# Router columns first: attention's last value columns moved into the steps of a search

## The chip, the core and the metric

The program runs on one core of one Trainium2 chip, as one launch. The metric is device time in microseconds. Below, PE is the matrix engine, DVE the vector engine, ACT the scalar engine, POOL the general engine, SP the queue that issues most transfers.

## What is computed

Three layers in a row, all in f32. Attention: 8 batches, 8 heads, 576 queries of 64 columns; keys and values are averaged over groups of 8 rows, so a query sees 72 of them. A mixture of 8 experts with a greedy assignment under a capacity of 576 tokens each. A gated feed-forward layer.

```python
attn = softmax(scale * q @ pool8(k).T); x = attn @ pool8(v)        # 4608 tokens x 512
logits = x @ w_gate                                                # 4608 x 8
for idx in argsort(-logits.flatten()):       # best pair first
    tok, e = idx // 8, idx % 8
    if assigned[tok] < 0 and counts[e] < 576: assigned[tok] = e; counts[e] += 1
out[mask_e] = relu(x[mask_e] @ w1[e]) @ w2[e]                      # each expert
return (sigmoid(out @ w_gate2) * (out @ w_val2)) @ w_out2
```

## The kernel before

The attention (`attention`, lines 242 to 603) works in 18 tiles of 256 tokens: two for each batch, and behind every fourth batch a mixed one (tiles 8 and 17) with the queries left over from four batches. A tile is cut into chunks of heads (line 294): packed tiles into three of 3, 3 and 2 heads, the first tile and the mixed ones into four of 2. A chunk has u units, one for each head and each of two query rows: 6 or 4. It goes through scores (PE, line 456, several chunks in one group, one score buffer), a maximum and a subtraction (DVE, 472 and 476), exp (ACT, 479), a transpose (PE, 492), a copy to SBUF (ACT, 500), values (PE, 517 and 512; 526 in mixed tiles), and then on DVE the sums (534, 535), the normalisation to `xt` (541) and the logits `lm` (547); the last chunk of a tile adds its logits up into `L` (550), and SP stores `xt` to `x_rows` (559, 563).

The router's logits come out of the same matmul as the values: the right-hand side `wv` has 73 columns for each head, 64 of the value, 8 of value times router weight, and a column of ones for the sum. In packed tiles one value matmul covers two units, so it streams 146 columns over weights of 108 rows and 128 columns (`eT`); a chunk of 6 units has four of them, one of 4 units has two, and a third of 73 columns. An f32 matmul shows as two instructions in the trace.

The order of all this is worked out by a planner, `Plan` (line 155): each piece is an `Op` with a cost for each engine, what it waits for, the buffer it makes and a rank. `Plan.run` takes, among the pieces that can start within 0.25 us of the earliest, the one with the lowest rank. Ranks go by the chunk's number, so the mixed tile 17 comes last. Buffers are counted by tag (line 270): one score buffer, two `aps` for values, four `qps`, three `xt`.

Behind the attention the router takes over. Keys for token columns 0 to 25 are made while the attention runs (598, 599), those of columns 26 to 35, which are tiles 13 to 17, behind it (603). Then come eight phases, one for each expert. In a phase (`Router.phase`, line 924) two searches of four steps each (`search`, 886) look for the threshold: DVE compares the keys with 15 thresholds (`C`), PE counts with 36 small matmuls, DVE finds the hits (`hit`, `fl`), PE turns them into the next thresholds. The generator yields before it counts (with a cost of 0.8) and after the hits (0.05). Behind the last step DVE writes `GE` and `EG`, the expert is chosen, its weights are loaded (`stg`), its slots are worked out and its rows of `x_rows` gathered (`xg`).

The first phase has nothing beside it. `experts` (line 1036) runs it in a loop; from its 17th step on, `heat` puts filler matmuls into PE's waits (lines 1251 to 1256). From the second phase on a search runs between the matmuls of the expert before. The memory of the attention (tile pools `acon`, `alod`, `awrk`, `apsm`) is given back when `attention` ends, and the pools of the experts lie in the same place; `cw` are buffers for the weights of the third layer, which SP starts to load at the start of `experts`.

Of the kernel before, what the change touches and what calls it, by code (L numbers as in the profile page):

```python
# [18 lines left out]
G = S // 8  # L19
N = B * S  # L20
DM = H * D
E = 8
# [132 lines left out]
class Plan(Flow):  # L155
# [9 lines left out]
    def op(self, lanes, f, after=(), reads=(), makes=None, rank=0, size=0, alone=False, rate=350e3, dmas=1):  # L165
        x = Op(lanes, f, [a for a in after if a is not None], list(reads), makes, rank)
        x.size, x.alone, x.rate, x.dmas = size, alone, rate, dmas
# [34 lines left out]
    def run(self):  # L202
        while self.todo:
# [38 lines left out]
def attention(tc, c, q, k, v, w_gate, xD, L, router, scr):  # L242
    nc = tc.nc
    ident = c["ident"]
    with ExitStack() as ctx:
# [24 lines left out]
        BUFS = dict(kv=6, q2=2, qps=4, sps=1, aps=2, mx=3, sd=3, e=7, eT=4, qT=5, rs=3, xt=3)  # L270
# [26 lines left out]
        NQ = len(chunks)  # L297
        fb = {b: first[ti] for ti, (n, b, jj) in enumerate(tiles) if b is not None and jj == 0}
# [106 lines left out]
        def plan_q(ti):  # L405
            n, b, jj = tiles[ti]
            base = first[ti]
# [24 lines left out]
        def plan_score(group):  # L432
# [24 lines left out]
            sc = fl.op({"tensor": 0.3 + 0.125 * at}, score, after=list(dict.fromkeys(need)), reads=read, makes=sps, rank=group[0] - 3)  # L457
            for y in group:
                score_of[y][1] = sc
            return score_of[group[0]]  # L460

        def plan_chunk(y, out):
# [5 lines left out]
            mx, sd, e, tps, eT, aps, rs = (Buf(m, None) for m in ("mx", "sd", "e", "qps", "eT", "aps", "rs"))  # L468
            sps, sc, at = score_of[y] if y in score_of else plan_score(group_of[y])
            S2 = lambda: sps.ap[:, :, G * at:G * (at + nh)].rearrange("p r (h k) -> p r h k", k=G)  # L470
            two = lambda ap: ap.rearrange("p (r h) k -> p r h k", r=2)
            m = fl.op({"vector": 0.07 + 72 * u / 960}, lambda eng: eng.tensor_reduce(tile_of(mx, work, [128, 6])[:, :u].rearrange("p (r h) -> p r h", r=2), S2(), axis=AX.X, op=OP.max),
                      after=[sc], makes=mx, rank=y - 3)
# [4 lines left out]
            s = fl.op({"vector": 0.07 + 72 * u / 960}, sub, after=[m], reads=[sps, mx], makes=sd, rank=y - 3)  # L478
            x = fl.op({"scalar": 0.13 + 72 * u / 1200}, lambda eng: eng.activation(tile_of(e, work, [128, 6, G])[:, :u], sd.ap[:, :u], AF.Exp),
                      after=[s], reads=[sd], makes=e, rank=y)  # L480
# [12 lines left out]
            tn = fl.op({"tensor": 0.109 * len(cuts)}, turn, after=[x], reads=[e], makes=tps, rank=y)  # L493

            def turned(eng):
                t = tile_of(eT, work, [108, 4, 128])
# [4 lines left out]
            tcp = fl.op({"scalar": 0.52}, turned, after=[tn], reads=[tps], makes=eT, rank=y)  # L501

            def values(eng):
                p = tile_of(aps, psum, [128, 6, 73])
                t = eT.ap
                count["av"] += 1
                if packed[ti]:
                    flat = wv[b % 2].rearrange("p w h d -> p (w h) d")
                    for a in range(0, u, 3):
# [28 lines left out]
            def norm(eng):  # L538
                if out.ap is None:
                    out.ap = work.tile([128, 2, H, D], F32, name="xt", bufs=3), work.tile([128, 2, H, E], F32, name="lm", bufs=3)  # L540
# [1297 lines left out]
```

## Time and profile before

| | us |
|---|---|
| median of 3 runs | 1505.7 (1504.81 to 1512.39) |
| the profiled execution | 1506.83 |
| its span | 1505.2 |
| PE busy in it | 1459.1 (97%) |
| DVE busy | 1059.7 (70%) |
| ACT busy | 537.8 (36%) |

The page cuts the span into 40 equal slices and gives the busy tenths of each engine and the clock that PE was granted. The chain that ended last is followed back from the last instruction; windows give busy times by stretch; groups by shape give the mean duration of one instruction. Lines are those of the kernel before; where a helper records the operations, all have line 615, and the tiles tell them apart.

### The profile page before, as it was taken

How to read it: one execution, taken by the hardware profiler on the slowest of the kernel's cores; microseconds unless marked ns; L12 is line 12 of the kernel's file. 1: busy time of each engine (PE TensorE's matmuls, PEld its weight loads, DVE VectorE, ACT ScalarE, POOL GpSimd, SP SyncE). 2: the span in 40 equal slices, each digit the busy share in tenths (PEclk: the TensorE clock that was granted, in tenths of full speed). 3: DMA queues.
4: the chain of work that ended last, by engine and by line, in shares of the span. 5: the costliest groups of instructions: out<-in, count | busy, mean ns of one | idle time of the engine just before them, and what ended most of it. 6: DMA issues, size and time to landing. Idle time of an engine off the chain costs nothing.

```text
span 1505.2 us, 27177 instructions
## 1 busy us (share of the span) xinstructions
PE 1459.1 (97%) x10625; PEld 1309.6 (87%) x10625; DVE 1059.7 (70%) x2344; ACT 537.8 (36%) x1063; POOL 395.5 (26%) x416
## 2 busy tenths in 40 slices
PE   8999799999999999998999999999999999999997
PEld 6898489999999999997888888888888899999996
DVE  6789788988899986247788755577455855574564
ACT  5665143444334444345334322232321322232221
POOL 5682042244333422154324210012000220011001
PEclk9999699999999999999999999999999999999999
DMA  9984336536554775047566564626544375555651
GB/s 331 311 305 140 116 125 211 187 111 210 182 192 134 247 239 188 24 152 292 218 238 227 205 221 150 234 110 231 191 166 182 112 293 192 227 212 226 247 196 43
DMA packets 109329, 294.22 MB, mean 195 GB/s; under 512 B 12588, under 2 KB 43344, under 8 KB 94992
## 3 DMA queue, kind: packets, MB, share of 16 engines
q1 hardware_dynamic: 101636, 270.48, 50.3%
q0 software_dynamic: 6496, 20.98, 4.2%
q8 instruction: 84, 1.38, 0.4%
q10 hardware_dynamic: 1068, 1.03, 0.3%
q14 instruction: 45, 0.37, 0.1%
HBM read 222.33 MB, written 66.08 MB: 192 GB/s over the span
## 4 chain that ended last, share of the span: by engine, by line
PE 82%; DVE 9%; DMA 4%; issue 2%; POOL 1%; SPq 1%; ACT 0%; POOLq 0%; ACTq 0%; DVEq 0%
PE pj L1675 19%; PE hps L615 12%; PE acc L615 12%; PE Yv L1577 7%; PE Yg L1577 7%; PE Zg L1577 5%; PE Xg L1577 5%; PE Xv L1577 5%; PE Zv L1577 5%; DMA kv<-in_v_dram 2%; PE rps L615 2%; PE aps L517 2%; DVE cx L615 1%; PE qps L492 1%; PE sps L456 1%
## 5 line engine op out<-in xcount | busy, mean ns | idle before, releaser
L615 PE MATMUL acc<-hh,w 128*128 128x288 f32 x1024 | 246.1, 305 | 0.0
L615 PE MATMUL hps<-xh,w 128*128 128x288 f32 x1024 | 234.8, 300 | 1.0 <-DVE hl L615 1.0
L1689 DVE TENSOR_TENSOR stg<-pj,stg 128x512 f32<-128x512 f32 x180 | 123.8, 689 | 109.1 <-PE pj L1675 108.2
L615 PEld LDWEIGHTS acc<-hh,w 128*128 128x128 f32 x1024 | 177.1, 189 | 0.2
L615 PEld LDWEIGHTS hps<-xh,w 128*128 128x128 f32 x1024 | 174.5, 189 | 1.9 <-DVE hl L615 1.4
L615 PE MATMUL acc<-hl,w 128*128 128x288 f32 x512 | 151.6, 296 | 0.9 <-DVE hl L615 0.9
L615 PE MATMUL hps<-xl,w 128*128 128x288 f32 x512 | 151.4, 296 | 0.1
L615 POOL TENSOR_TENSOR w<-stg,w 128x512 fp32r<-128x512 f32 (+1 forms) x81 | 119.8, 1493 | 116.0 <-ACT w L615 109.9
L615 ACT ACTIVATE hh<-hps 128x288 fp32r<-128x288 f32 x128 | 52.6, 411 | 252.8 <-PE hps L615 237.8
L1577 PE MATMUL Yg<-w 128*128 128x512 f32 (+1 forms) x540 | 126.5, 369 | 3.7 <-ACT w L1475 3.7
L1577 PE MATMUL Yv<-w 128*128 128x512 f32 (+1 forms) x540 | 126.5, 369 | 0.1
L1577 PEld LDWEIGHTS Yg<-w 128*128 128x128 f32 x540 | 99.6, 188 | 19.9 <-ACT w L1475 4.1
L1577 PEld LDWEIGHTS Yv<-w 128*128 128x128 f32 x540 | 99.5, 189 | 13.6 <-DVE vc L1613 0.8
L615 POOL DMA_INDIRECT xg<-x_rows,idxs x48 | 46.0, 959 | 221.9 <-PE hps L615 70.2
L1675 PE MATMUL pj<-woh,xg 128*128 128x512 f32 x396 | 98.4, 390 | 0.7 <-DVE woh L1544 0.7
L1675 PE MATMUL pj<-woh,cw 128*128 128x512 f32 x396 | 98.7, 390 | 0.0
L615 PEld LDWEIGHTS acc<-hl,w 128*128 128x128 f32 x512 | 97.1, 190 | 1.1 <-DVE hl L615 1.1
L1643 ACT ACTIVATE sg<-sg 128x512 f32<-128x512 f32 (+1 forms) x90 | 53.0, 589 | 122.6 <-DVE sg L1614 73.9
L615 PEld LDWEIGHTS hps<-xl,w 128*128 128x128 f32 x512 | 96.6, 189 | 0.3 <-DVE xl L615 0.3
L615 DVE SCALAR_TENSOR_TENSOR hl<-hps,hh 128x288 fp32r<-128x288 f32 x128 | 57.4, 452 | 53.2 <-ACT hh L615 52.1
L615 ACT ACTIVATE w<-stg 128x512 fp32r<-128x512 f32 (+1 forms) x138 | 81.0, 638 | 34.5 <-DVE rem L615 28.9
L1675 PEld LDWEIGHTS pj<-woh,xg 128*128 128x128 f32 x396 | 74.0, 188 | 15.8 <-DVE woh L1544 1.1
(280 smaller groups left out, 2954.3 us busy)
## 6 DMA issues: line engine op xcount, KB each, us to landing
w<-w_split SPq DMA_DIRECT2D x84, 1024.0 KB
stg<-in_moe_w_dram SPq DMA_DIRECT2D x30, 1024.0 KB
w_split<-w SPq DMA_DIRECT2D x21, 1024.0 KB
woh<-wo_split SPq DMA_DIRECT2D x24, 512.0 KB
wr<-wo_split SPq DMA_DIRECT2D x12, 1024.0 KB
kv<-in_k_dram SPq DMA_DIRECT2D x12, 768.0 KB
kv<-in_v_dram SPq DMA_DIRECT2D x12, 768.0 KB
x_cols<-x SPq DMA_DIRECT2D x16, 576.0 KB
```

Source lines behind the costliest of these rows:

```text
L456: eng.matmul(p[cs, r, G * j:G * j + G], t.ap[rs, h % 4, cs], kpT[rs, b if b is not None else 4 * n + 2 * c + r, h], start=True, stop=True)
L492: eng.transpose(p[:z, j], flat[:, a:a + z], ident)
L517: eng.matmul(p[:, a + s:a + s + 2], t[:, j + s], flat[:, x0:x1 + 1:x1 - x0], start=a + s == 0, stop=True, skip_group_check=True)
L615: r = f(*args, **kw)
L1577: eng.matmul(t, W(a, k), X(b, k), start=first and n == 0, stop=n == 5, skip_group_check=True)
L1643: x = fl.op(A, lambda eng: eng.activation(T(g), T(g), AF.Sigmoid), after=[op], rank=rank)
L1675: eng.matmul(self.tile(ps), G(a), W(b), start=n == 0, stop=n == 5)
L1689: y = fl.op({"vector": 0.69}, lambda eng: eng.tensor_tensor(A(), self.tile(ps), A(), op=OP.add), after=[x, st["acc", u, i]], reads=[ps], r ...
```

## The change

Tiles 13 to 16 (batches 6 and 7) are `halved`. In each of their chunks the values matmul takes the columns 64 to 72 alone, 9 for each unit and so 18 for each matmul, into one `aps` for the whole tile. Sums, reciprocals and logits are then done once for a tile, on 16 units. `eT` of these chunks is kept in buffers of the raw loads (`kv`). The 64 value columns become operations of their own that are marked `late` (`plan_rest`): for each tile 11 matmuls, 16 scalings on ACT (one for each unit, with the reciprocal as scale) and the store. The planner may place them, but it stops when only late ones are left. The rest goes out behind the attention's last piece: matmuls up to the 15th (`burst(15)`), then the keys of columns 26 to 35, then one or two matmuls in each of the fifteen yields of the first phase's two searches, and what is then left at once. Scalings and stores follow their matmuls in the same list.

The mixed tile's ranks are lowered by 6, beside those of tile 15. `xt` has six buffers. The first phase's searches run inside `attention` now, with their PSUM in the `aps` buffers and a pool `router0` of their own on the other side of the memory; `experts` goes on behind them, and `heat` plans its fillers at 0.216 us.

```diff
-        while self.todo:
+        while not all(x.late for x in self.todo):
...
-        BUFS = dict(kv=6, q2=2, qps=4, sps=1, aps=2, mx=3, sd=3, e=7, eT=4, qT=5, rs=3, xt=3)
+        BUFS = dict(kv=6, q2=2, qps=4, sps=1, aps=2, mx=3, sd=3, e=7, eT=4, qT=5, rs=3, xt=6, rl=4)
...
+        rk = lambda y: y - 6 if chunks[y][0] == 17 else y
+        halved = {13, 14, 15, 16}
...
+        def plan_rest(ti, own, rs, out, n2, store):
+            done = []
+            for triples, h0, nh, u, y in pend[ti]:
+                ps, last = Buf("qps", None), n2
+                parts = []
+
+                def one(eng, parts=parts, ps=ps, triples=triples, y=y, nh=nh):
+                    if not parts:
+                        parts.extend(triples(tile_of(ps, psum, [128, 6, 64]), own.part[y], 0, 64, nh))
+                        parts.reverse()
+                    o, i, m, new = parts.pop()
+                    eng.matmul(o, i, m, start=new, stop=True, skip_group_check=True)
+                for j in range(u // 3 * 2 + (u % 3 > 0)):
+                    last = fl.op({"tensor": 0.223}, one, after=[last], makes=ps, rank=500 + y, late=True)
+
+                def scale(eng, ps=ps, h0=h0, nh=nh, u=u):
+                    for a in range(u):
+                        r, h = a // nh, h0 + a % nh
+                        eng.activation(out.ap[0][:, r, h], ps.ap[:, a], AF.Identity, scale=rs.ap[:, r * H + h:r * H + h + 1])
+                done.append(fl.op({"scalar": 0.18 * u}, scale, after=[last], reads=[ps], rank=500 + y, late=True))
+            fl.op({"sync": 0.6}, store, after=done, rank=500, size=524288, late=True)
...
             def values(eng):
+                count["av"] += 1
+                if own:
+                    p = tile_of(aps, psum, [128, 2 * H, 9])
+                    for o, i, m, new in triples(p, own.part[y], 64, 73, H, h0):
+                        eng.matmul(o, i, m, start=new and h0 == 0, stop=True, skip_group_check=True)
+                    return
...
-            av = R["av", y] = fl.op({"tensor": 0.248 * (len(cuts) // 2 * 2) + 0.175 * (len(cuts) % 2) if packed[ti] else u * (0.175 if b is not None else 0.2)}, values,
-                                    after=[tcp] + vals, reads=[eT], makes=aps, rank=y)
+            av = R["av", y] = fl.op({"tensor": 0.115 * len(cuts) if own else 0.248 * (len(cuts) // 2 * 2) + 0.175 * (len(cuts) % 2) if packed[ti] else u * (0.175 if b is not None else 0.2)}, values,
+                                    after=[tcp] + vals, reads=[eT], makes=aps, rank=rk(y))
+
+            if own:
+                pend.setdefault(ti, []).append((triples, h0, nh, u, y))
+                if h0 + nh < H:
+                    return
+                nu, c0, hs = 2 * H, 0, slice(0, H)
...
         fl.run()
         for _ in consts:
             pass
+        rest = deque(fl.todo)
+
+        def burst(n):
+            while rest and (n > 0 or "tensor" not in rest[0].lanes):
+                x = rest.popleft()
+                lane, = x.lanes
+                x.f(getattr(nc, lane))
+                n -= lane == "tensor"
...
+        router.nc, router.psum, router.spare = Clock(nc), Banks, Banks
+        burst(15)
         router.keys(0, 26, 36)
+        router.steps = router.run()
+        for i in range(15):
+            cost, _ = next(router.steps)
+            burst(2 if cost > 0.1 else 1)
+        burst(len(rest))
...
-        rt = router.run()
+        rt = router.steps
...
-        n = 0
         while st["phase"] < 1:
-            n += 1
-            if n > 16:
-                heat(wait["ready"] - 0.1, 0.43 if n < 25 else 0.216)
+            heat(wait["ready"] - 0.1)
             route()
```

## Rows read from the trace of the kernel before

**Rows 1.** The page, section 2: busy tenths in 40 slices; granted clock

```profile
PE   8999799999999999998999999999999999999997
...
PEclk9999699999999999999999999999999999999999
```

**Rows 2.** Windows: stretch, length, busy us of PE, PEld, DVE, ACT, POOL; clock; DMA

```profile
142.00:149.00 7.00, 7.00 (x122) 6.51 (x124) 6.34 (x21) 4.62 (x11) 0.00 (x0) 1.00 0.18 75
...
128.00:159.70 31.70, 28.92 (x467) 25.36 (x467) 27.88 (x101) 17.44 (x40) 0.00 (x0) 1.00 0.29 107
```

**Rows 3.** Chain that ended last, 0 to 260 us: start, us, what

```profile
156.28 0.60 ACT eT L500
156.93 0.73 PE aps L526 x16
...
158.96 0.75 PE aps L526 x16
...
179.62 0.70 PE rps L615 x7
```

**Rows 4.** Timeline of the search: start, us, engine, line, operation, tiles

```profile
165.98 0.20 PE L615 MATMUL rps<-trw,fl 128*128 128x15 bf16 x1 [0.26 <-DVE hit L615]
...
166.67 1.02 PE L615 MATMUL acc<-EoU,C 128*15 128x8 bf16 x35
...
167.95 0.19 PE L615 MATMUL rps<-trw,fl 128*128 128x15 bf16 x1 [0.26 <-DVE hit L615]
```

**Rows 5.** Groups by shape, 128 to 161.2 us: busy us, mean ns; idle before

```profile
L541 DVE TENSOR_TENSOR xt<-aps,rs 128x384 f32<-128x384 f32 x8 | 4.5, 558 | 0.3
...
L541 DVE TENSOR_TENSOR xt<-aps,rs 128x256 f32<-128x256 f32 x8 | 3.4, 424 | 0.2
...
L547 DVE TENSOR_TENSOR lm<-aps,rs 128x48 f32<-128x48 f32 x8 | 1.6, 194 | 0.0
...
L500 ACT ACTIVATE eT<-qps 72x128 f32<-72x128 f32 x4 | 1.1, 264 | 0.0
```

**Rows 6.** Chain around 147 us, then the timeline of weight loads there

```profile
146.78 0.50 PE aps L517 x4
147.28 0.18 PE aps L512 x2
...
147.12 0.19 PEld L512 LDWEIGHTS aps<-wv,eT 72*128 72x128 f32 x1
147.23 0.30 PEld L517 LDWEIGHTS aps<-wv,eT 108*128 108x128 f32 x2
```

**Rows 7.** Timeline behind T0: last logits, last counts of step one

```profile
160.70 0.38 DVE L550 TENSOR_REDUCE L<-lm 128x16 f32<-128x128 f32 x1
...
163.25 0.39 PE L615 MATMUL acc<-EoU,C 128*15 128x8 bf16 x10 [1.70 <-DVE EoU L881]
```

**Rows 8.** Who waited for whom: us in total, times, longest

```profile
SPq L615 <- DMA x_rows<-xt: 1.6, 1, 1.6
...
PE acc L615 <- DVE lm L547: 1.0, 1, 1.0
```

**Rows 9.** Timeline of SP's issues

```profile
160.60 2.45 SPq L563 DMA_DIRECT2D x_rows<-xt  x4
164.99 1.30 SPq L615 DMA_DIRECT2D cw<-in_moe_w_gate_dram  x3
182.45 0.98 SPq L615 DMA_DIRECT2D stg<-in_moe_w_dram  x2
```

**Rows 10.** Timeline at the end of the search

```profile
178.51 0.29 DVE L615 TENSOR_TENSOR GE<-kl,rps 128x36 bf16<-128x36 f32 x2 [0.29 <-PE rps L615]
```

**Rows 11.** Windows of 1 us, columns as in rows 2

```profile
156.00:157.00 1.00, 0.26 (x4) 0.07 (x4) 0.97 (x5) 0.72 (x2) 0.00 (x0) 1.00 0.75 307
...
167.00:168.00 1.00, 0.74 (x29) 0.64 (x25) 0.23 (x3) 0.00 (x0) 0.00 (x0) 0.50 0.93 381
184.00:185.00 1.00, 1.00 (x5) 0.30 (x3) 0.96 (x3) 0.00 (x0) 0.00 (x0) 0.81 0.70 240
```

More of the change, by code (lines that the diff above doesn't have):

```diff
@@ L163, in __init__, with op @@
         self.flights = [0.0] * 8
[L165 removed]
+    def op(self, lanes, f, after=(), reads=(), makes=None, rank=0, size=0, alone=False, rate=350e3, dmas=1, late=False):
         x = Op(lanes, f, [a for a in after if a is not None], list(reads), makes, rank)
[L167 removed]
+        x.size, x.alone, x.rate, x.dmas, x.late = size, alone, rate, dmas, late
         for b in x.reads:
@@ L456, in score @@
                             eng.matmul(p[cs, r, G * j:G * j + G], t.ap[rs, h % 4, cs], kpT[rs, b if b is not None else 4 * n + 2 * c + r, h], start=True, stop=True)
-            sc = fl.op({"tensor": 0.3 + 0.125 * at}, score, after=list(dict.fromkeys(need)), reads=read, makes=sps, rank=group[0] - 3)
+            sc = fl.op({"tensor": 0.3 + 0.125 * at}, score, after=list(dict.fromkeys(need)), reads=read, makes=sps, rank=rk(group[0]) - 3)
             for y in group:
@@ L519, in values @@
+                    for o, i, m, new in triples(p, t, 0, 73, nh):
+                        eng.matmul(o, i, m, start=new, stop=True, skip_group_check=True)
                 else:
@@ new lines, in sums, with begin @@
+            def sums(eng):
+                r = tile_of(rs, work, [128, 2 * H if own else 6])
+                eng.tensor_scalar(r[:, :nu], aps.ap[:, :nu, c0 + 8], 1e-9, None, op0=OP.add)
+                eng.reciprocal(r[:, :nu], r[:, :nu])
+            sm = fl.op({"vector": 0.3}, sums, after=[av], makes=rs, rank=rk(y))
+            def begin():
+                if out.ap is None:
+                    out.ap = work.tile([128, 2, H, D], F32, name="xt", bufs=BUFS["xt"]), work.tile([128, 2, H, E], F32, name="lm", bufs=BUFS["xt"])
@@ L538, in norm @@
             def norm(eng):
-                if out.ap is None:
-                    out.ap = work.tile([128, 2, H, D], F32, name="xt", bufs=3), work.tile([128, 2, H, E], F32, name="lm", bufs=3)
+                begin()
                 eng.tensor_tensor(out.ap[0][:, :, h0:h0 + nh, :], two(aps.ap[:, :u, 0:64]),
                                   rs.ap[:, :u].rearrange("p (r h) -> p r h", r=2)[:, :, :, None].to_broadcast([128, 2, nh, 64]), op=OP.mult)
-            n1 = fl.op({"vector": 0.07 + 64 * u / 960}, norm, after=[sm], makes=out, rank=y)
+            if not own:
+                n1 = fl.op({"vector": 0.07 + 64 * u / 960}, norm, after=[sm], makes=out, rank=rk(y))
@@ L549, in logits @@
                 if h0 + nh == H:
                     eng.tensor_reduce(L[:, 2 * ti:2 * ti + 2, :], lm.rearrange("p r h e -> p r e h"), axis=AX.X, op=OP.add)
-            n2 = fl.op({"vector": 0.12 if h0 + nh < H else 0.45}, logits, after=[n1], reads=[aps, rs], rank=y)
+            n2 = fl.op({"vector": 0.12 if h0 + nh < H else 0.55 if own else 0.45}, logits, after=[sm if own else n1], reads=[aps, rs], makes=out, rank=rk(y))
             if h0 + nh < H:
@@ L564, in store @@
                                       xt[64 * s:64 * s + 64, r].rearrange("p h d -> p (h d)"))
-            fl.op({"sync": 0.6 if b is not None else 2.4}, store, after=[n2], reads=[out], rank=y, size=524288, dmas=1 if b is not None else 4)
+            if own:
+                plan_rest(ti, own, rs, out, n2, store)
+                return
+            fl.op({"sync": 0.6 if b is not None else 2.4}, store, after=[n2], reads=[out], rank=rk(y), size=524288, dmas=1 if b is not None else 4)
         def loads_of(b):
```

71 lines of the change are left out of this document (45 added, 26 removed).

## The prediction

> **What bounds the kernel now.** The page comes first. In its 40 slices of 37.6 us the granted TensorE clock is at 9 tenths or more everywhere but in the fifth, 150 to 188 us, and PE is busy for 8 tenths or more of every slice behind that but the last [rows 1]. The fifth holds the end of the attention and the first search, and the change adds no work behind it. What happens before only moves the rest, so I follow the points that come ahead of it: the last value matmul of the attention (call it T0), the first hit, the last hit, and GE, the first step after the search.
>
> The stretches come second. From 128 us, where the last five tiles begin, to T0 at 159.7 PE is busy 28.9 of 31.7 us, DVE 27.9, ACT 17.4 [rows 2]. From 142 to 149 PE leaves no gap at all [rows 2]. Its gaps lie behind 149. Third, the chain of waits says which: the last tile (17, the mixed one) runs alone, and each of its chunks goes transpose, ACT copy (156.28), values, 2.0 us apart (values at 156.93 and 158.96) [rows 3], PE standing still during the copies. So there are two limits: PE's own work, and the latency of the mixed tile.
>
> Then the first search, from T0 to 178.5. It is a pure latency chain: PE counts, DVE hit, PE threshold, DVE compare, 1.97 us a step (thresholds at 165.98 and 167.95) [rows 4], eight steps. ACT does nothing in it.
>
> **DVE's share.** In tiles 13 to 16 twelve chunks lose their sums, normalisation and logits. That is 8 wide normalisations of 558 ns and 4 narrow ones of 424, for each wide chunk a logit product of 194 [rows 5], and two small operations for the sum. Counted at 1.0 us a wide chunk and 0.85 a narrow one that is 8 x 1.0 + 4 x 0.85 = 11.4 us, against four single sums and products on 16 heads at an estimated 0.6 each: DVE loses about 9 us of its 27.9. It then no longer limits anything before T0. Sixty-four normalisations of 64 columns go to ACT, which is idle in the search; the nearest row, an ACT copy of 128 columns, takes 264 ns [rows 5], so 0.15 to 0.25 us each, 10 to 16 us in a stretch of 18.
>
> **PE's share.** A value matmul goes from 146 moving columns to 18, and one of 128 follows later. What does a short one cost? Each f32 matmul is two passes, each with its own weight load. Four passes over 146 columns take 0.50 us, two over 73 take 0.18 (0.125 and 0.09 a pass) [rows 6]. So half the columns save a quarter. The reason stands in the loads: the load behind the short pass starts 0.11 us after the one before it (147.12, 147.23) [rows 6], however short the pass. I therefore price the 18-column matmul at 2 x 0.11 = 0.22 us against 0.25, and the third one of a narrow chunk at 0.22 against 0.18: 40 x 0.03 - 4 x 0.04 = 1.0 us saved, not the 5.7 that the planner's new cost (0.115 a matmul) assumes. Bounds: 0 and 5.7. The Trainium skill ("TensorE: Matmul & The Clock Gate", section "LDWEIGHTS (loading the stationary operand)") speaks against the change in the same place: a load's time goes by the columns of the weights, by its formula 107 ns for 128. By that rule the estimate would be 0.21 us a matmul and 1.4 us saved; the trace's 0.11 agrees.
>
> The separate matmuls of 128 columns lie between the two rows: 0.23 us, 44 of them, 10.1 us of new PE work.
>
> **T0.** The ranks put the mixed tile beside tiles 15 and 16, so its latency is covered and the gaps behind 149 can be filled. PE's visible idle time from 128 to T0 is 31.7 - 28.9 = 2.8 us; the pipeline's drain after each wait counts as busy too (a threshold matmul of 15 columns shows 0.20 us [rows 4]), so up to about twice that can come back. I take 3.5 and the 1.0 from above. Against that, the late operations stay candidates in the planner's loop: wherever its plan has PE idle for over 0.25 us, it puts one in. Its plan prices the short matmuls at half of what they cost, so some of these gaps won't exist on the chip. I take 8 of the 44 there (bounds 0 and 20), and half of their 1.8 us as a delay. T0 comes 3.5 + 1.0 - 0.9 = 3.6 us earlier; bounds 0.5 and, with the cheap matmul, 8.
>
> **The first hit.** Before, the last counts of the first step run at 163.25, after the keys of columns 26 to 35, which start after the logits at 160.70 [rows 7]. From T0 that is 3.6 us, and PE is nearly free in it. Now 15 late matmuls stand first in PE's order, 15 x 0.23 = 3.45 us, then the 26 counts that need no new keys (0.8, at the pace of [rows 4]), and only then the last ten: at 4.25, 0.7 us later than before. That is the cost of a cover that is almost long enough.
>
> **The steps.** One late matmul stands between the counts and the threshold, two between threshold and counts. The holes are there: from the end of a count group (about 167.69) to the threshold at 167.95 is 0.26 us, against 0.23; from the threshold at 165.98 to the counts at 166.6 is 0.63, against 0.46 and a first load of 0.11 [rows 4]. Cost at full clock: 0, at most 0.1 a step.
>
> **The end of the search.** 36 late matmuls are left at T0 by my count. The first burst and the fifteen steps take 15 + 22 = 37 of them, so the last go out with the last hits. Behind them on ACT come the scales of their chunk, behind these on SP the last store. Who waits for that? The tiles of the next stage lie where the attention's were. The rows show what the first user of such memory waits for: the first load of cw waited 1.6 us for the stores of xt [rows 8]; it was issued at 164.99, 1.9 us after the last of the four stores had been [rows 9]. The first count matmul likewise waited for the last reader of the attention's PSUM [rows 8]. GE is the first write into such a region on DVE, and lies on the path: at 178.51, straight behind the last threshold [rows 10], with the stores landed long before. Now the last store is issued about 1.2 us after the last late matmul (scales and a hop) and lands 2.3 us behind that. A last matmul at the seventh hit makes GE about 1.5 us late, one at the eighth 3.5, a full remainder of 44 about 6; one at the sixth costs nothing. I take 1.5. The loads of cw also move behind that store on SP and stand ahead of the expert's weights there; before, they were issued 17 us ahead of them (164.99 and 182.45) [rows 9], and the weights go out 4 us after GE, so I count 0, and 1 to 2 us where the store itself is late.
>
> **The clock.** It is full at 156, half (1.2 GHz) at 167 although PE shows 74% busy there, and comes back at 184 [rows 11]. At 156 to 157 it stayed full with PE 26% busy between busier microseconds [rows 11]. With the late matmuls in the holes I expect full clock to the end of the search. The gain is small. The chain of a step hangs on DVE and on hops more than on the array; the seven wide products behind GE take 0.70 us at half clock [rows 3], and I take 0.4 us for these and the small ones around them.
>
> **Sum**, from the profiled execution's own 1506.8 us (span 1505.2, 1.6 around it): -3.6 + 0.7 + 0 + 1.5 - 0.4 = -1.8, 1505.0. That execution lay 1.1 above the median of the three runs, 1505.7; from that median: 1503.9.
>
> **Rivals.**
> *The attention's end shrinks by far more.* If the short matmul costs what the planner says, and the score and DVE chain alone set T0, T0 comes up to 8 us earlier, the rest as above: -8 + 0.7 + 1.5 - 0.4 = -6.2, 1499.5. For it: DVE loses a third of its work. Against it: the weight loads [rows 6]. Chance 0.2.
> *The last store holds GE (slower).* If the planner finds few gaps, 40 or more late matmuls are left, the last seven go out behind the last hit, and GE waits 4 to 6 us; T0 gains 4 at most, the first hit loses 0.7: -4 + 0.7 + 5.6 - 0.4 = +1.9, 1507.6. It decides from 37 left on: with T0 earlier by only 1.5 and GE late by 3.5 it is +2.3. For it: the wait on x_rows that cw shows [rows 8]. Against it: the idle time behind 149 gives the planner gaps. Chance 0.25.
> *The clock falls in the search.* Late matmuls then take 0.46 us: each step grows by 0.2 + 0.3 us, eight steps 4 us, and the filler matmuls behind the search, now planned at 0.216 us and taking 0.43, push the path by some 3 more: +4 to +6, 1510. The Trainium skill (same page, section "What's actually happening") says that throttled is the default state and activity releases it; a search that is mostly small products might not count as such. The trace's search at half clock agrees with that, and no run here shows counts and late matmuls mixed. Chance 0.07.
> *The change doesn't do what it says*: the planner puts most of the late matmuls back before T0. Then T0 moves by 0 to 1, GE waits for nothing: 1505.5. Chance 0.08.
>
> **How the numbers follow.** The forecast has 0.4. What moves is a stretch of some 50 us out of 1505, so every case but the ends of the first and third lies within 0.5% (7.5 us, about what a measurement of this kernel can tell from no change): faster by more 0.08, within 0.88, slower by more 0.04. The range leaves out the ends of those two cases: 1498.3 to 1509.
>
> **What would show it.** T0 at 155 to 157.5 and the mixed tile's values before tile 16's; short value matmuls 0.21 to 0.23 us apart; the last counts of the first step 4.2 us behind T0 (3.6 before); search steps still 1.97; granted clock 1.0 in the search; GE right behind the last threshold, or, if the store holds it, DVE idle there with the landing of x_rows as the releaser; the loads of the expert's weights 22.5 to 26 us behind T0 (22.8 before). The prediction is wrong if T0 moves by over 6 us, if the steps get longer, or if anything behind 200 us changes its own length.

## The result and the profile after

| | before | changed |
|---|---|---|
| median of 9 runs each, us | 1507.2 (1504.8 to 1512.4) | 1520.0 (1516.5 to 1523.2) |
| ratio | | 1.008, 95% interval 1.0065 to 1.0094 |
| profiled execution, us (span) | 1506.8 (1505.2) | 1520.4 (1518.7) |

The changed kernel is some 12 us slower: slower by over 0.5%, to which I had given 0.04. To say where, I lay the points of the prediction one behind the other in both profiles. They begin at three transposes of keys and values at 86 us, up to which both run the same plan (86.46 before, 85.88 after); that takes out half a microsecond by which the executions differ ahead of it. The timeline of PE at that point, before and changed (start, us, line, operation, tiles):

```profile
86.46 0.55 PE L359 MATMUL qps<-identf,kv 128*128 128x128 f32 x3
```
```profile
85.88 0.55 PE L362 MATMUL qps<-identf,kv 128*128 128x128 f32 x3
```

In us:

| stretch | before | changed | difference |
|---|---|---|---|
| transposes at 86 to T0 (159.69; 161.46) | 73.23 | 75.58 | +2.35 |
| T0 to the first hit (163.78; 166.40) | 4.09 | 4.94 | +0.85 |
| first hit to the eighth (178.05; 184.99) | 14.27 | 18.59 | +4.32 |
| eighth hit to GE (178.51; 188.78) | 0.46 | 3.79 | +3.33 |
| GE to the first expert matmul (194.78; 207.87) | 16.27 | 19.09 | +2.82 |
| from there to the end | 1310.4 | 1310.8 | +0.4 |

Five losses, then, all ahead of 208 us. The page of the changed kernel, section 2 (busy tenths in 40 slices; granted clock), answers [rows 1]:

```profile
PE   8999999999999999998999999999999999999997
...
PEclk9999799999999999999999999999999999999999
```

It looks better than before: the fifth slice has a clock of 7 tenths, where it was 6, and PE is busier. A slice of 38 us is too coarse here. The windows (stretch, length, busy us of PE, PEld, DVE, ACT, POOL; clock; DMA) answer [rows 2, 11]:

```profile
128.00:161.50 33.50, 32.61 (x494) 30.01 (x493) 21.21 (x70) 19.75 (x49) 0.00 (x0) 0.90 0.13 39
134.00:141.00 7.00, 7.00 (x110) 6.75 (x108) 5.03 (x15) 5.57 (x14) 0.00 (x0) 0.97 0.26 76
141.00:149.00 8.00, 8.00 (x77) 7.34 (x78) 2.69 (x10) 2.71 (x5) 0.00 (x0) 0.60 0.00 1
161.00:168.00 7.00, 7.00 (x112) 6.70 (x112) 4.29 (x24) 6.89 (x35) 0.00 (x0) 1.00 0.51 152
168.00:186.00 18.00, 17.73 (x282) 15.44 (x279) 6.67 (x34) 6.58 (x30) 0.00 (x0) 0.50 0.17 67
186.00:200.00 14.00, 11.25 (x78) 5.00 (x77) 7.01 (x34) 0.00 (x0) 0.00 (x0) 0.67 0.74 265
```

The clock column is the news. Before, it stayed full to T0 [rows 2]; now it falls to half for most of 141 to 149 (below, such a drop is called a fall), with PE busy all the time and DVE and ACT mostly idle, and again from 168 on. The timeline of PE shows what PE did at the first fall:

```profile
136.98 0.54 PE L523 MATMUL qps<-identf,e 128*108 128x128 f32 x3
137.35 6.41 PE L559 MATMUL aps<-wv,kv 108*128 108x18 f32 x44
143.61 3.64 PE L523 MATMUL qps<-identf,e 128*108 128x128 f32 x16
```

All 22 short value matmuls of tiles 13 and 14 (44 passes) stand in one row, and the clock falls inside it, by 1-us windows between 140 and 141 us. The 16 transposes behind it then take 3.64 us.

The search, same view, answering [rows 4, 7]:

```profile
160.66 0.80 PE L559 MATMUL aps<-wv,kv 108*128 108x18 f32 x6
161.31 4.04 PE L476 MATMUL qps<-wv,kv 108*128 108x128 f32 x34
165.34 1.02 PE L702 MATMUL aps<-EoU,C 128*15 128x8 bf16 x35
166.29 0.49 PE L476 MATMUL qps<-wv,kv 108*128 108x128 f32 x2
166.62 0.18 PE L702 MATMUL aps<-trw,fl 128*128 128x15 bf16 x1
166.66 0.69 PE L476 MATMUL qps<-wv,kv 108*128 108x128 f32 x4
167.34 1.02 PE L702 MATMUL aps<-EoU,C 128*15 128x8 bf16 x35
...
171.09 0.79 PE L476 MATMUL qps<-wv,kv 108*128 108x128 f32 x2
171.68 0.22 PE L702 MATMUL aps<-trw,fl 128*128 128x15 bf16 x1
171.75 1.20 PE L476 MATMUL qps<-wv,kv 108*128 108x128 f32 x4
172.94 1.02 PE L702 MATMUL aps<-EoU,C 128*15 128x8 bf16 x35
```

Ahead of the counts stand 17 late matmuls (34 passes). At full clock a step is 2.0 us (hits at 166.40 and 168.39); at half clock the late matmuls take 0.79 and 1.20 in place of 0.49 and 0.69, and steps are 2.7 to 2.8. Counts take 1.02 at either clock. Behind the search, the timeline of DVE and two pieces of the chain of waits (start, us, what), answering [rows 8, 10]:

```profile
184.99 0.16 DVE L702 TENSOR_SCALAR_CACHE_REDUCE hit<-aps 15x8 f32<-15x8 f32 x1 [1.08 <-PE aps L702]
188.78 0.29 DVE L702 TENSOR_TENSOR GE<-kl,rps 128x36 bf16<-128x36 f32 x2 [3.62 <-DMA x_rows<-xt]
```
```profile
182.99 0.96 PE qps L476 x4
...
184.93 3.67 DMA x_rows<-xt
```

GE waits for the last store: its last matmul ends at 183.95, scalings take 1.0 us, the store lands 3.67 us after its issue. On SP the loads of `cw` and of the expert's weights follow it, answering [rows 9]:

```profile
188.72 1.28 SPq L702 DMA_DIRECT2D cw<-in_moe_w_gate_dram  x3
192.76 1.01 SPq L702 DMA_DIRECT2D stg<-in_moe_w_dram  x2
```

The expert's weights go out 4.0 us behind GE, as before. And between GE and the slots the fillers, changed kernel first, then the kernel before:

```profile
193.05 5.33 PE L702 MATMUL hps<-C,onesb 128*128 128x512 bf16 x19
198.31 1.07 PE L702 MATMUL rps<-R,OHL 128*32 128x36 bf16 x36
```
```profile
181.86 3.33 PE L615 MATMUL hps<-C,onesb 128*128 128x512 bf16 x9
185.45 1.07 PE L615 MATMUL rps<-R,OHL 128*32 128x36 bf16 x36 [0.26 <-DVE OHL L615]
```

The fillers are planned for full clock, and the clock comes back at 195.3 us: the six ahead of this row (2.76 us for six) and about five of the nineteen run at half. The slots' product comes 9.53 us behind GE and not 6.94.

### The profile page after: what moved, and what is told of

Same layout as the page of the kernel before. It is cut to its first block, busy times and chain, and to the rows that moved or that the text cites. A ratio compares the mean times of both kernels' runs of the same rounds, so it can differ in the third digit from the quotient of the medians.

```text
span 1518.7 us, 27401 instructions
## 1 busy us (share of the span) xinstructions
PE 1478.8 (97%) x10728; PEld 1326.4 (87%) x10728; DVE 1052.6 (69%) x2308; ACT 552.1 (36%) x1127; POOL 394.6 (26%) x416
## 4 chain that ended last, share of the span: by engine, by line
PE 83%; DVE 8%; DMA 4%; issue 2%; POOL 1%; ACT 1%; SPq 1%; POOLq 0%; ACTq 0%; DVEq 0%
PE pj L1759 19%; PE hps L702 12%; PE acc L702 11%; PE Yg L1661 7%; PE Yv L1661 7%; PE Zg L1661 5%; PE Zv L1661 5%; PE Xg L1661 5%; PE Xv L1661 5%; DMA kv<-in_v_dram 2%; PE rps L702 2%; DVE cx L702 1%; PE qps L476 1%; PE aps L565 1%; PE qps L523 1%
## 5 line engine op out<-in xcount | busy, mean ns | idle before, releaser
L1759 PEld LDWEIGHTS pj<-woh,xg 128*128 128x128 f32 x396 | 74.0, 188 | 15.9 <-DVE woh L1628 1.1
```

The source lines that it names most:

```text
L1759: eng.matmul(self.tile(ps), G(a), W(b), start=n == 0, stop=n == 5)
```

## The experiments

My theory behind these traces: the row of short matmuls costs the attention its clock, the mix of counts and late matmuls costs the search its clock, and the last store holds GE. Rivals stand with each run. One table first: time against the kernel before on the same chip, then from each profile the stretches of the table above (in us) and, by 1-us windows, the time at half clock between 100 us and T0.

| run | ratio (95%) | 86 to T0 | half clock there | T0 to first hit | to eighth hit | to GE | to expert |
|---|---|---|---|---|---|---|---|
| kernel before | 1 | 73.2 | 0 | 4.1 | 14.3 | 0.5 | 16.3 |
| changed | 1.008 (1.0065 to 1.0094) | 75.6 | 6.8 | 4.9 | 18.6 | 3.8 | 19.1 |
| e18_again | 1.0070 (1.0052 to 1.0088) | 76.0 | 6.8 | 4.9 | 18.6 | 3.2 | 20.1 |
| e1_first | 1.0092 (1.0071 to 1.0113) | 75.3 | 6.8 | 10.4 | 14.2 | 0.5 | 20.6 |
| e4_none | 1.0002 (0.9992 to 1.0013) | 74.5 | 0 | 4.2 | 14.3 | 0.5 | 17.8 |
| e5_wide | 1.0060 (1.0041 to 1.0078) | 71.1 | 0 | 4.9 | 17.3 | 3.8 | 18.0 |
| e16_wide | 1.0069 (1.0052 to 1.0085) | 77.0 | 10.2 | 4.9 | 18.6 | 3.8 | 19.9 |
| e7_ge | 1.0042 (1.0029 to 1.0055) | 74.9 | 6.8 | 4.9 | 18.4 | 0.5 | 17.8 |
| e8_cols | 1.0043 (1.0028 to 1.0058) | 73.1 | 3.4 | 5.0 | 14.5 | 3.5 | 18.3 |
| e3_rank | 1.0077 (1.0044 to 1.0109) | 82.5 | 24.2 | 9.1 | 16.8 | 0.8 | 19.9 |
| e6_price | 1.0099 (1.0065 to 1.0133) | 79.4 | 20.5 | 4.9 | 18.0 | 5.7 | 17.9 |
| e9_all | 1.0014 (1.0003 to 1.0025) | 77.0 | 10.2 | 4.9 | 14.5 | 0.5 | 17.9 |
| e10_late2 | 1.0026 (1.0013 to 1.0039) | 73.6 | 0 | 4.9 | 14.3 | 0.5 | 20.0 |
| e11_early2 | 1.0027 (1.0017 to 1.0038) | 77.2 | 10.2 | 4.6 | 14.3 | 0.5 | 18.1 |
| e12_mix | 1.0033 (1.0020 to 1.0046) | 74.7 | 0 | 4.9 | 15.9 | 0.5 | 18.1 |
| e13_bcols | 1.0024 (1.0010 to 1.0039) | 73.1 | 1.4 | 4.3 | 18.1 | 0.5 | 16.4 |
| e14_xt | 1.0085 (1.0070 to 1.0099) | 74.8 | 10.2 | 5.2 | 17.8 | 3.2 | 19.8 |
| e15_best | 1.0042 (1.0026 to 1.0058) | 70.7 | 0 | 5.2 | 14.5 | 0.5 | 20.2 |
| e17_conv | 1.0039 (1.0024 to 1.0054) | 72.6 | 0 | 5.2 | 14.5 | 0.5 | 20.7 |

Behind the first expert matmul the profiles take 1308 to 1315 us (1318 and 1316 in the last two), which no run explains, so a single profile's total says less than its stretches. The first stretch varies too: in the six profiles that have the changed kernel's order and full clock up to 139 us, the last transposes of keys and values come 46.0 to 47.8 us behind those at 86. Differences under 2 us in "86 to T0" can be chance.

**Nothing halved (e4_none).** Does the split carry the loss, or what came with it?

```diff
-        halved = {13, 14, 15, 16}
+        halved = set()
```

> No tile is halved; ranks, buffers, the search inside the attention and the filler price of the change stay. Theory (the split of the value matmuls carries the loss): clock full from 141 to 149, the last value matmul of the attention at 158 to 161, steps 1.97, GE straight behind the last threshold; 1505 to 1510 us, of which up to 2 us above the kernel before come from fillers planned at 0.216 us while the clock is half. Rival (the search's new place or the ranks carry it): GE waits or the attention ends late here too, 1513 us or more.

As the theory had it: the time of the kernel before, steps 1.97, GE free. Of the rest of the change two small costs may show: T0 1.2 us later (within what executions differ by) and GE to the expert 1.5 longer, which fits fillers at 0.216 while the clock is half.

**The row of short matmuls (e5_wide, e16_wide, e10_late2, e11_early2).** Wider ones, in the same order:

```diff
-                    p = tile_of(aps, psum, [128, 2 * H, 9])
-                    for o, i, m, new in triples(p, own.part[y], 64, 73, H, h0):
+                    p = tile_of(aps, psum, [128, 2 * H, 31])
+                    for o, i, m, new in triples(p, own.part[y], 42, 73, H, h0):
...
-                nu, c0, hs = 2 * H, 0, slice(0, H)
+                nu, c0, hs = 2 * H, 22, slice(0, H)
```

> The short value matmuls of tiles 13 to 16 take 31 columns for each unit in place of 9, so 62 moving columns in a matmul and not 18; the 22 more are not used. Order and number of instructions are those of the changed kernel. Theory (the row of 44 passes with 18 columns each lets the clock fall at 140.8): a pass still costs 0.11 us, the clock stays at 1.00 from 141 to 149, and the attention's last value matmul comes about 2.8 us earlier (158.7 against 161.5), and so does the end: about 2.8 us faster than the changed kernel. Rival (the clock falls because PE ran for long without a gap): it falls at the same place or sooner, and nothing is gained, or 0 to 1 us lost to the longer stream.

> The version with 31 columns a unit in the short value matmuls and no other edit, once more: the clock stayed full from 141 to 149 us in its first profile, but fell there in the profile of the three edits together, whose attention is the same. Theory 1 (62 columns are near what keeps the clock, and it goes either way from one execution to the next): times of two kinds some 4 us apart, the lower near 1.004 to 1.005 of the kernel before. Theory 2 (62 columns don't matter, the first profile was chance): the clock falls, and the times are those of the changed kernel, 1.008.

Timeline of PE and window of the first, then the window of the second:

```profile
136.37 5.00 PE L559 MATMUL aps<-wv,kv 108*128 108x62 f32 x44
141.20 1.94 PE L523 MATMUL qps<-identf,e 128*108 128x128 f32 x16
...
156.51 0.82 PE L559 MATMUL aps<-wv,kv 108*128 108x62 f32 x6
```
```profile
141.00:149.00 8.00, 7.89 (x156) 1.00 0.01 2
```
```profile
141.00:149.00 8.00, 8.00 (x71) 0.58 0.08 25
```

The first ran as the theory said, with 0.11 us a pass and the transposes in 1.94; the second fell, having fallen at 125 to 129 us already. So the width alone isn't shown to be the cure. The times point to two kinds of execution: of the eight of this kernel five lie 6 to 8 us above the median of the kernel before on their chip and three 12 to 15, and the profiles are of the lowest and the highest; all 13 of the changed kernel lie 9 to 16 above. The two halves of the change settle the place: `halved = {15, 16}` and `halved = {13, 14}`.

> Only tiles 15 and 16 are halved; 13 and 14 keep their 146-column value matmuls. Theory (the attention's fall of the clock comes from the 22 short matmuls of tiles 13 and 14 in a row at 137.35 us): that row streams 146 columns now, the clock stays full from 137 to 149, the attention's last value matmul lies 72 to 74 us behind the transposes at 86 us (75.6 in the changed kernel, 73.2 before); 15 late matmuls are left and all go ahead of the counts, so steps are 1.97 us and GE waits for no store: 1507 to 1511 us. Rival (any short matmul, or the rest of the change, lets the clock fall): it falls here too, a few us later, and the attention ends no earlier than in the changed kernel.

> The complement: only tiles 13 and 14 are halved. Theory: the row of 22 short matmuls stands, the clock falls at 138 to 141 us, the attention's last value matmul lies 75 to 76.5 us behind the transposes at 86 us; with few late matmuls left the steps are 1.97 us and GE isn't held: 1510 to 1514. Rival (the row isn't the cause): clock full from 137 to 149, as with tiles 15 and 16, and the same time as there.

Timeline of PE and window of 15 and 16 alone, then of 13 and 14 alone:

```profile
135.60 2.16 PE L565 MATMUL aps<-wv,eT 108*128 108x146 f32 x16
```
```profile
141.00:149.00 8.00, 7.33 (x107) 1.00 0.28 115
```
```profile
137.70 6.27 PE L559 MATMUL aps<-wv,kv 108*128 108x18 f32 x44
143.82 2.57 PE L523 MATMUL qps<-identf,e 128*108 128x128 f32 x11
```
```profile
141.00:149.00 8.00, 8.00 (x77) 0.57 0.02 5
```

The fall comes with that row. Over all profiles: with tiles 13 and 14 at 18 columns the clock fell between 130 and 150 us in 9 of 9 (e18_again is the changed kernel once more, below), with 146 columns in 0 of 5, with 62 in 2 of 5. In some of these the order is another: in e14_xt (18 columns), e15_best and e17_conv (both 62) the passes stand in rows of 16, 14 and 14 with other work between, in e3_rank (18) in rows of 30 and 14. The row of 44 at 62 columns fell in 2 of 3. Three profiles (e11_early2, e16_wide, e9_all) show a fall of 3.4 us at 124 to 125 us too, ahead of any short matmul, behind 1 to 2 us in which PE mostly waited, as it also did there in profiles without that fall. So these short matmuls bring the fall between 130 and 150 us; what in them does (the columns, the loads, the order) stays open.

The price of the fall is read from the row's start to T0, in profiles with the changed kernel's order: 21.0 us with full clock (136.37 to 157.33, e5_wide), 22.4 with 3.4 us at half clock (e8_cols), 24.1 to 24.2 with 6.8 (changed, e18_again, e1_first, e7_ge, and with 62 columns e9_all and e16_wide). The fall costs the changed kernel 3.1 us. The 4.5 us between it and e5_wide in the table hold 1.3 more that arise ahead of the row, at full clock in both. And the price hardly shows in the times of the two halves, which are alike (1.0026 and 1.0027): in their profiles T0 is 3.6 us apart, but 15 and 16 alone lose 1.9 of it between GE and the expert, and more behind, for reasons that no run shows.

> The changed kernel as it is, once more, for a second profile and a ratio on the same chip. Theory (the fall of the clock in the attention belongs to this order of matmuls and is no chance of one execution): the clock falls again for some 3.4 to 6.8 us between 138 and 149 us and again in the search by 170 us; ratio to the kernel before 1.007 to 1.009. Rival (chance): full clock from 137 to 149 us and a time 3 to 5 us lower.

The clock fell again, at 141 us and in the search at 168, and the ratio is 1.0070: no chance of one execution.

**Late matmuls ahead (e1_first).** `burst(15)` becomes `burst(len(rest))`.

> All late matmuls go out in one row ahead of the counts, none in the search. Theory (the late matmuls in the steps cost 0.8 us a step once the clock has fallen, and their last store holds GE 3.3 us): 72 passes at 0.115 us put the first hit at about 170.8 (changed kernel 166.4), bare steps are 1.97 us at either clock, so the last hit is at about 184.7 (185.0), but the last store has landed some 10 us before, and GE comes at 185.2 instead of 188.8: 3 to 4 us faster than the changed kernel. Rival (the steps are long for another reason, such as the counts' new PSUM buffers or the half clock alone): the steps stay at 2.7 to 2.8, the last hit is at 190.4, GE at 191, 2 us slower than the changed kernel.

The places came as expected: hits 1.97 us apart, eighth hit 184.92, GE 185.39. The total didn't follow: no faster than the changed kernel. The 5.5 us of burst ahead of the first hit ate most of the 7.7 won in the steps and at GE, and GE to the expert took 20.6 us, 1.5 more. The mixture makes the steps long, but taking it out is no cure.

**GE's memory (e7_ge).**

```diff
-                router.pool = rsb
+                router.rsb = rsb
...
+        if k == 0:
+            self.pool = self.rsb
         OHL = self.t([128, NT // 2, LO, 2], BF16, "OHL")
```

> GE, EG and the small tiles behind them in the first phase lie in the pool that was opened ahead of the attention, not in memory that the attention gave back. Theory (GE waits for the last store only because its pool lies where xt lay): GE runs at about 185.5, straight behind the last threshold, in place of 188.8; 3.3 us faster than the changed kernel. Rival (something else is late next: PSUM of the fillers and thresholds behind the scalings, the order on SP, the gather): GE comes early, but the first expert matmul moves by under 1 us.

```profile
183.24 0.16 DVE L702 TENSOR_SCALAR_CACHE_REDUCE hit<-aps 15x8 f32<-15x8 f32 x1 [1.09 <-PE aps L702]
183.69 0.29 DVE L702 TENSOR_TENSOR GE<-kl,rps 128x36 bf16<-128x36 f32 x2 [0.29 <-PE rps L702]
```

Shown: GE waits for the store through its memory alone. Some 4 to 6 us came back (1.0042 against 1.0070 and 1.008). 3.3 of them are GE's, 1.3 lie between GE and the expert, where the half clock lasts 3.7 us behind GE and not 6.5.

**Columns in the counts (e8_cols, e13_bcols).** Both have this edit, the second on the kernel before:

```diff
-                                 EoU[:, g * c:g * c + g], start=c == 0, ...
+                                 EoU[:, c, None, :].to_broadcast([128, 6, E]), start=c == 0, ...   # k == 0
```

> The 36 count matmuls of a step of the first phase stream 48 columns each in place of 8: the same 8 columns six times, of which the first copy is used. Theory (the clock falls in the search because PE, though never idle, streams few columns there, and the count's 25 ns are set by something else than its columns): counts still take 0.9 to 1.0 us, the clock stays full, the steps are 2.0 us in place of 2.7 to 2.8, fillers take what they are planned at; last hit 4 to 5 us nearer to the first one than in the changed kernel (18.6), GE to the first expert matmul 17 us (19.1); together 6 us faster than the changed kernel. The hold on GE stays, some 3 us. Rival 1 (the clock falls for another reason): 48 columns at half clock take 40 ns, counts 1.5 us, steps 3.2, 3 to 4 us slower than the changed kernel. Rival 2 (48 columns cost time at full clock too): steps 2.3 or more, gain under 3 us.

> The kernel before, with 48 columns in the first phase's counts in place of 8, and nothing else. Theory (columns streamed keep the clock): the clock stays full from 160 to 184, where it was half; the steps remain 1.97, since they hang on hops, and the products and fillers behind GE gain 0.4 to 1 us: same as the kernel before within 1 us. Rival (the clock falls since PE stands still for 0.9 us in each step here): counts take 1.5 us at half clock, steps 2.4, 3 to 4 us slower.

Timeline of PE and window of the changed kernel's search with 48 columns, then of that of the kernel before with 48:

```profile
168.43 0.49 PE L476 MATMUL qps<-wv,kv 108*128 108x128 f32 x2
168.80 0.69 PE L476 MATMUL qps<-wv,kv 108*128 108x128 f32 x4
169.48 1.04 PE L702 MATMUL aps<-EoU,C 128*15 128x48 bf16 x35
```
```profile
168.00:186.00 18.00, 14.06 (x257) 0.94 0.30 104
```
```profile
166.00 0.21 PE L615 MATMUL acc<-EoU,C 128*15 128x48 bf16 x1 [0.44 <-DVE C L615]
166.07 1.56 PE L615 MATMUL acc<-EoU,C 128*15 128x48 bf16 x35
```
```profile
168.00:186.00 18.00, 13.67 (x213) 0.55 0.08 30
```

In the changed kernel the clock stays to 183 us, and steps are 2.0 to the end of the search. So the fall of the clock, not the late matmuls' place, makes the steps long. The other profiles agree: where late matmuls stand in the steps, the clock stayed full through the search in 4 of 4 with 48 columns (e8_cols, e9_all, e15_best, e17_conv) and was half in part of it in 8 of 8 with 8. On the kernel before the rival held: with the holes empty the clock is half all the same, and the wide counts then cost 0.55 us a step. (In e12_mix, where late matmuls end ahead of the search, steps 6 to 8 fell to that state too.)

**Ranks and price (e3_rank, e6_price).** `rk = lambda y: y`, and 0.22 for 0.115 in the planner.

> The mixed tile's ranks are those of the kernel before; all else is the changed kernel. Theory (the lowered ranks pull the mixed tile's queries ahead and so delay the transposes of the last batches' keys and values, 133.3 against 130.4 us): these come back to about 130.5, and the attention's last value matmul comes 1 to 2 us earlier, if the row of short matmuls still lets the clock fall. Rival (as I predicted, the ranks cover the latency of the mixed tile, worth 3.5 us): it runs alone again, with PE idle in each copy, and the attention ends 2 to 3.5 us later than in the changed kernel.

> The planner is told 0.22 us for a short value matmul, as the trace shows it, in place of 0.115; all else is the changed kernel. Theory (the wrong price lines the short matmuls up: 22 in a row from 137.35 us): its plan puts mixed chunks and scores between them, the clock falls later, shorter or not at all, the last value matmul comes 1 to 3 us earlier. Rival (the row stands because the shifted values of the last batch arrive only at 137 to 139 us): the same row, the same fall of the clock, no gain.

Both theories fell: the clock was half for 24.2 and 20.5 us ahead of T0, and the attention ended later. In e6_price the row of 44 passes stood all the same, as its rival had it, so the wrong price isn't what lines it up. What the ranks are worth is therefore open; that the last transposes stay at 132.9 us with the old ranks says they aren't what delays them.

**The xt buffers (e14_xt).** The delay comes with nothing halved as well, so I looked at the rest:

```diff
-        BUFS = dict(..., rs=3, xt=6, rl=4)
+        BUFS = dict(..., rs=3, xt=3, xh=4, rl=4)
...
-            out = Buf("xt", None)
+            out = Buf("xh" if ti in halved else "xt", None)
```

> The six xt buffers of the change are split: three for the tiles up to 12 and the mixed ones, as before, and four of their own for the halved tiles; all else is the changed kernel. Theory (the additional xt buffers change the plan from 85 us on and so delay the last batches' transposes: 119.3 us there in the version with nothing halved and 118.7 in the changed kernel, against 111.2 before): the fourth last of these comes 7 us earlier, the last one 1 to 3 us earlier; the attention ends 1 to 3 us earlier than the changed kernel's 75.6 us behind the transposes at 86, if the clock falls as long as there. Rival (the lateness comes from the halving itself or from the transfers): the transposes stay where they are.

The fourth last transposes of keys and values, in the changed kernel, in this one, and in the kernel before:

```profile
118.69 0.55 PE L362 MATMUL qps<-identf,kv 128*128 128x128 f32 x3
```
```profile
109.91 0.49 PE L362 MATMUL qps<-identf,kv 128*128 128x128 f32 x3
```
```profile
111.24 0.49 PE L359 MATMUL qps<-identf,kv 128*128 128x128 f32 x3
```

Shown: the additional buffers let the planner take up other work first. The last transposes lie 43.2 us behind those at 86, as before (44.0), and not 47.4 (43.3 and 45.2 in e15_best and e17_conv, which have this edit too). What that is worth at T0 isn't settled. It gains 2.2 us against e9_all and e16_wide, which also had 10.2 us at half clock; but with full clock T0 lies at 70.7 and 72.6 with the buffers split, at 71.1 without. The time gained nothing (1.0085).

**All cures together (e9_all, e12_mix, e15_best, e17_conv).** e9_all has e5, e7 and e8; e12_mix the same without tiles 13 and 14; e15_best is e9_all with e14's buffers and the first `conv(1)` of the third layer's weights moved behind the first phase; e17_conv moves that on behind the first expert's splits.

> Three edits on the changed kernel together: 31 columns a unit in the short value matmuls, 48 columns in the first phase's counts, GE and the small tiles behind it in the pool opened ahead of the attention. Theory (the three causes are separate): 5 us (the short row, as measured) and 3 to 6 us (GE, as measured alone) and 4 to 5 us in the steps, less what two of them count twice (the fillers at half clock): 10 to 14 us faster than the changed kernel, 1506 to 1510, level with the kernel before or 1 to 3 us faster. Rival (the clock falls in the search all the same): 1511 to 1515.

> Tiles 15 and 16 halved, 48 columns in the first phase's counts, GE and the small tiles behind it in the pool opened ahead of the attention. Theory: no fall of the clock in the attention nor in the search, steps 2.0, fillers at their planned 0.216: 1 to 3 us faster than tiles 15 and 16 alone, level with the kernel before or up to 2 us faster. Rival (the clock falls in one of the two stretches all the same): 2 to 5 us slower than the kernel before.

> All that has helped, together: split xt buffers, 31 columns a unit in the short value matmuls, 48 columns in the first phase's counts, GE and the small tiles behind it in the pool opened ahead of the attention, and the first loads of the third layer's weights behind the first phase, so that they no longer stand ahead of the first expert's weights on SP. Theory: from the transposes at 86 us, 71 to the attention's end, 4.9 to the first hit, 14.5 to the last, 0.5 to GE, 16.3 to the first expert matmul: 107.2 against 108.3 before, so level with the kernel before or 1 to 3 us faster, if the clock stays full in the attention. Rival (62 columns don't hold the clock there): 2 to 4 us slower than the kernel before.

> The version with all edits together, but the first loads of the third layer's weights go out only behind the first expert's weights are split (there they went out straight behind these weights' loads and shared the transfer engines with them: the first weights came 11.7 us behind GE, 9.3 before). Theory: the attention's end, the search and GE as there (70.7, 5.2, 14.5 and 0.5 us), GE to the first expert matmul 16 to 17 us in place of 20.2: 107 to 108 us from the transposes at 86 us, 108.3 before: level with the kernel before, at best 1 us faster, and 3 us faster than the version with all edits. Rival (the last store, or the rows' gather, sets the first expert matmul): still 19 us or more, and 1.004 of the kernel before.

e9_all and e12_mix were to be level with the kernel before and are 2 and 5 us slower: the profile of the first fell in the attention, that of the second in the search. In e15_best every stretch up to GE came out as expected, and GE lies 90.8 us behind the transposes, 1.2 us earlier than before (92.05); but in e17_conv, the same up to there, it lies at 92.7, so no gain is shown. What was gained in e15_best is given back behind GE. Timeline: the moved loads go out right behind the expert's, and the gather's rows are waited for.

```profile
180.75 1.70 SPq L702 DMA_DIRECT2D cw<-in_moe_w_gate_dram  x3
...
192.07 0.55 PE L702 MATMUL acc<-identf,xg 96*128 96x96 f32 x4 [3.41 <-DMA xg<-x_rows,idxs]
```

e17_conv didn't move them as meant (cw out at 183.34, straight behind the expert's at 182.28), so that collision is read from the trace but not tried. No version beat the kernel before; of those with halved tiles e9_all comes nearest.

## Why the prediction was wrong, step by step

The step that failed is the clock: I took it as full up to the end of the search and priced T0 with it. It was half for 6.8 us ahead of T0 and from 168 to 195 us, which cost 3.1 us in the attention, 4.3 in the steps and, with fillers planned for full clock, 2.6 of the 2.8 behind GE. The hold on GE, 3.3 us for 1.5, was a term of the right kind that I sized too small.

- **DVE's share**: right in kind. DVE is busy 21.2 of 33.5 us, where it was 27.9 of 31.7: 6.7 less, not 9. The 64 scalings take 0.22 us of ACT each (0.15 to 0.25 forecast), 13.9 us together, although a single one lasts 353 ns, since they overlap; the group by shape, answering [rows 5] (busy us, mean ns, idle before):

```profile
L483 ACT ACTIVATE xt<-qps,rl 128x64 f32<-128x64 f32 x64 | 13.9, 353 | 10.4 <-PE qps L476 5.8 <-PE aps L702 4.6
```
- **PE's share**: right. 22 short matmuls in 5.00 us are 0.23 each (0.22 forecast), though the planner has 0.115 (the 5.00 us are those of e5_wide, at full clock); 17 late ones in 3.9 us on the chain are 0.23. The Trainium skill's rule on loads ("TensorE: Matmul & The Clock Gate", section "LDWEIGHTS (loading the stationary operand)"), by which a load's time goes by the columns of the weights, agrees with that.
- **T0**: forecast 3.6 earlier with bounds 0.5 and 8, measured 2.35 later. I priced the attention at full clock throughout and bounded it nowhere for half: 3.1 us, and the sign. At full clock it would have been 0.8 earlier (2.1 in e5_wide), a mis-sized term within its bounds. The mixed tile's latency was covered, and its values do come before tile 16's, as forecast; but PE's idle time from 128 us to T0 went from 2.8 to 0.9 us, so 1.9 came back at most where I took 3.5. The xt buffers, which move the transposes, I had named in no term. Eight of the 44 late matmuls were placed by the planner, as I took it, six ahead of T0 and two behind it; the eight were a guess between 0 and 20, so that is luck.
- **First hit**: 0.85 for 0.7, by the burst as described; the planner's two stand in it too.
- **Steps**: 2.0 at full clock, cost 0.02, as forecast, and 14.5 over the search in e8_cols. The condition, full clock, failed, not the fit.
- **End of the search**: right mechanism, and the last matmul did go out behind the seventh hit. The mis-sized term is the landing: 3.67 us (3.41 in e8_cols) where I had 2.3. The stores behind T0 in the kernel before are of 128 KB each, this one is of 512. At full clock GE still waited 3.3 (e8_cols). 3.3 for 1.5.
- **The clock**: forecast full, -0.4. It fell at 168: +4.3 in the steps, +2.8 in fillers and what hangs on them. The rival on it (chance 0.07) had both terms, 4 and some 3. Its 4 is partly luck: eight steps of 0.5 forecast, six steps of 0.7 to 0.8 measured. The Trainium skill (same page, section "What's actually happening") says that throttled is the default and that the state goes by how busy PE has been; PE busy for 7.00 of 7.00 us ahead of the first fall shows that the profile's busy share is no stand-in for that here.
- **The rivals** were summed one at a time, each with the gain at T0. Two came true together and that gain didn't: 0.85 + 4.3 + 3.3 + 2.8 + 2.35 = 13.6, with -0.6 ahead and +0.4 behind the 13.5 us between the spans. My range ended at 1509 because I had treated them as exclusive and left out their ends.

## What to carry to other kernels

A matmul that is cut to few columns saves little where its weight load is the price (0.23 us against 0.25 here), and a row of such matmuls can cost the clock of the work behind it: read the granted clock of a stretch as part of its cost, and bound a change there at half clock too. Sum the rivals that one cause can set off together. Price a loss from a point just ahead of it: two executions of one order differed by up to 1.8 us before they got there. A buffer count in a planned kernel is an edit to its order, far ahead of where the buffer is used.

## What the runs showed of the hardware

- 35 count matmuls take 1.02 us with 8 columns at either clock, 1.04 with 48 at full clock, and 1.56 with 48 at half.
- The clock fell to half while PE left no gap, in the attention (134 to 141 us, 7.00 of 7.00 us busy) and in the search (161 to 168). It stayed full with PE as busy in the kernel before (142 to 149, 7.00 of 7.00).
- At half clock 16 transposes took 3.64 us, at full clock 1.94.
- A store of 512 KB landed 3.67 us after its issue with nothing else of size under way (3.41 in e8_cols).
